# Moving the start addresses of TensorE's operands, and reading one weight with a step of two

## The chip, the core and the metric

The kernel runs on one core of one Trainium2 chip. The metric is the device time of one execution in microseconds; the figure for a kernel is the median of its runs. The kernel before takes 816.12 us (two runs, 815.71 and 816.52). The profiled execution shown here took 816.59 us.

## The reference

Three blocks in a row on 2304 tokens (batch 4 times 576) of width 512, all float32.

```python
# 1 attention with random features, 8 heads of 64, 128 features
h = omega @ (x * 64**-0.25) - |x|**2 / 2;  phi = exp(h - max(h)) / sqrt(128)      # for q and k
out = (phi_q @ (phi_k.T @ v)) / (phi_q @ sum(phi_k) + 1e-6)
# 2 feed-forward, 512 -> 2048 -> 512
x = softplus(x @ w_in) @ w_out
# 3 gated feed-forward, 512 -> 1024 -> 1024 -> 512
x = (((x @ w1) * (x @ w2)) @ w3) @ w_out2
```

## The kernel before

A float32 product is made of three products of `float32r` parts: an operand x is split into hi (x rounded by a copy to `float32r`) and lo (x minus hi), and `mm3` (L95 to L98) issues hi·hi, hi·lo and lo·hi into one accumulator. In each matmul one operand is the **stationary** one (128x128, loaded by a LDWEIGHTS that the trace shows under PEld), the other the **moving** one (256, 384 or 512 columns). In `mm3` the arguments `a` are the stationary parts and `b` the moving ones, so the three matmuls take stationary hi, hi, lo and moving hi, lo, hi.

The stages, in order of time:

- **Attention**: projections of k and q on omega (256 columns, stationary `kt` or `qt`, moving `om`), small float32 products, and transposes.
- **Up1** (class `Up1`, base `Quad`): x @ w_in in a scheme of seven products per 2x2 block. Stationary are the weight parts `hi`, `lo`, `thi`, `tlo` from pool `J_`; moving are token blocks of 384 columns from pools `X0` and `X1`. 1008 matmuls.
- **down** (function `down`): g @ w_out. Stationary is `w_out` in `X0`; moving are `dhi` and `dlo`, blocks of 512 columns (the last chunk 256) split from `dn` in pool `M_`. 768 matmuls of 512 columns and 192 of 256.
- **Up2**: as Up1, with the columns of w1 and w2. 1008 matmuls.
- **fold** (function `fold`, L878): w3 @ w_out2 is multiplied out first, as 8 row blocks. Stationary are w3's parts in `J_`, moving the 512 columns of w_out2 in `X1` (`spare` for the last of 8 blocks). 192 matmuls.
- **last** (function `narrow`): the gated product times the folded weight. Stationary and moving both lie in `X0` and `X1`. 504 matmuls of 384 columns.

SBUF is given out by pools, each a row of equal slots. The helper `mt` (L83) takes a slot of pool `M_` (14 slots of 2048 bytes in each partition), `jt` (L86) one of `J_` (8 slots of 4096 bytes). In the built program every operand of a `float32r` matmul, stationary or moving, starts at a multiple of 128 bytes. `lined` (L281) and the tile `edge` (L262) pad other tiles so that this holds.

The order of the instructions on each engine is set when the program is written (a list of small operations is pumped between matmuls at fixed rates, `step`); loads and stores go through SP's and ACT's DMA queues. The weights are laid out on the host (`_layout`); w3 arrives as rows of 1024 words, eight blocks of 128 one behind the other, and `fold` reads block i as `a:a + 128` with `a = 128 * i`.

Of the kernel before, what the change touches and what calls it, by code (L numbers as in the profile page):

```python
# [19 lines left out]
F32 = mybir.dt.float32  # L20
FR = mybir.dt.float32r
# [10 lines left out]
KD, NF, NJ = DM // 128, FF1 // 128, FF2 // 128  # L32
# [30 lines left out]
FILL = [18, 19, 20]  # L63
URGENT = 300
LINE = 32


@with_exitstack
def body(ctx: ExitStack, tc: tile.TileContext, q, k, k_rest, v, v_rest, om_t, w_in, w_out, w12, w3, wo, out):
    nc = tc.nc  # L70
    cp = ctx.enter_context(tc.tile_pool(name="cp", bufs=1))
    sm = ctx.enter_context(tc.tile_pool(name="sm", bufs=1))
    M_ = ctx.enter_context(tc.tile_pool(name="M_", bufs=14))
    L_ = ctx.enter_context(tc.tile_pool(name="L_", bufs=2))
    T_ = ctx.enter_context(tc.tile_pool(name="T_", bufs=4))
    J_ = ctx.enter_context(tc.tile_pool(name="J_", bufs=8))
# [3 lines left out]
    def ps():  # L80
        return ps_.tile([128, 512], F32, tag="ps", name="ps")

    def mt(n=512, dt=F32, name="m"):  # L83
        return M_.tile([128, n], dt, tag="m", name=name)

    def jt(name):  # L86
        return J_.tile([128, 1024], FR, tag="j", name=name)

    def tt(name):
        return T_.tile([128, 1024], F32, tag="t", name=name)  # L90
# [1 line left out]
    def matmul(o, a, b, start, stop, **kw):  # L92
        nc.tensor.matmul(out=o, lhsT=a, rhs=b, start=start, stop=stop, **kw)  # L93

    def mm3(o, ahi, alo, bhi, blo, first, last, **kw):  # L95
        matmul(o, ahi, bhi, first, False, **kw)
        matmul(o, ahi, blo, False, False, **kw)
        matmul(o, alo, bhi, False, last, **kw)  # L98
# [139 lines left out]
    def step(rate):  # L238
        due[0] += rate
        while due[0] > 0:  # L240
            if not pump_one():
                due[0] = min(due[0], 2.0)
                break
            due[0] -= 1

    def until(done):
        while not done():
            assert pump_one()
# [6 lines left out]
    for x in range(2):  # L255
        nc.vector.memset(bias[:, x:x + 1], BIAS * (2 * x - 1))
    win = [Job(w_in[i], 1024, jt, "J", True) for i in range(NF // 2)]
    w12_j = [Job(w12[i], 1024, jt, "J", True) for i in range(NJ)]


    edge = ctx.enter_context(tc.tile_pool(name="edge", bufs=1, side="right"))
    nc.gpsimd.memset(edge.tile([128, 24], F32, name="edge"), 0.0)  # L262
    qstack, kstack, x0stack = ExitStack(), ExitStack(), ExitStack()
    Q_ = qstack.enter_context(tc.tile_pool(name="Q_", bufs=1))
    K_ = kstack.enter_context(tc.tile_pool(name="K_", bufs=1, side="right"))
# [15 lines left out]
    def lined(pool, n, **kw):  # L281
        return pool.tile([128, -(-n // LINE) * LINE], F32, **kw)[:, :n]

# [68 lines left out]
    def k_feat_rest(r):  # L352
        kpr[r] = mt(name="kpr").rearrange("p (h m) -> p h m", h=4)
        p = project(lambda p: [krest[:, r, p, :]])
        waiting.append(lambda: features(*p, kpr[r]))
        flush(0)
# [118 lines left out]
    class Quad:  # L475
# [21 lines left out]
        def add(self, y, bank, name):  # L497
            z = mt(N, name=name)
            with tc.high_priority(URGENT):
                nc.vector.tensor_tensor(out=z, in0=bank, in1=y, op=ALU.add)  # L500
            return z

        def begin_parts(self):
            p6 = mt(N, name="p6")
            b1 = self.product("t2", "s2")
            with tc.high_priority(URGENT):
                nc.scalar.copy(out=p6, in_=b1)  # L507
            yield
            self.b2 = self.product("t3", "s3")
            yield  # L510
            self.b3 = self.product("t1", "s1")
            yield
            self.b0 = self.product("b11", "a11")
            self.u2 = self.add(p6, self.b0, "u2")
            u3 = self.add(self.u2, self.b2, "u3")
            self.c22 = self.add(u3, self.b3, "c22")
# [242 lines left out]
    for s in range(NW):  # L759
        n = min(WB, NF * 512 - WB * s)  # L760
# [63 lines left out]
    made, w34, xn = {}, {}, {}  # L824
# [41 lines left out]
    def w3_ops(j):  # L866
        return halves(w3f[j], 2, 2, "J", jt, ("w3", j))
# [10 lines left out]
    def fold(j):  # L878
        until(lambda: ("w3", j) in made)
        acc = ps()  # L880
        hi, lo = made["w3", j]
        for i in range(NJ):
            until(lambda: ("wo", i) in made)
            a = 128 * i
            mm3(acc, hi[:, a:a + 128], lo[:, a:a + 128], *made["wo", i], i == 0, i == NJ - 1)
            step(FOLD_RATE)
        o = mt(name="w34")
        with tc.high_priority(URGENT):
            nc.scalar.copy(out=o, in_=acc)
        free["J"] += 2  # L890
        return o
# [206 lines left out]
    for n, j in enumerate(order):  # L1098
        if 0 < n < NJ - 1:
            queue[:0] = w3_late.pop() + w3_next(n + 2)  # L1100
        rows[j] = fold(j)
        if n % 2:
            queue[:0] = w34_ops(n // 2, rows[order[n - 1]], rows[j])
# [8 lines left out]
def _layout(i):  # L1112
    import numpy as np

    def words(a):
        return np.ascontiguousarray(a).view(np.int64)

    q = i["q"].transpose(1, 3, 0, 2).reshape(4, 128, NT // 128, 128).transpose(2, 1, 0, 3)
    k = i["k"].transpose(0, 1, 3, 2).reshape(B, 2, 2, 128, S)
    k_main = k[..., :512].reshape(2 * B, 2, 128, 512).transpose(0, 2, 1, 3)  # L1120
    k_rest = k[..., 512:].reshape(B // 2, 2, 2, 2, 128, 64).transpose(4, 0, 2, 3, 1, 5).reshape(128, B, 2, 128)
    v = np.ones((B, 2, S, 4, D + 1), i["v"].dtype)
    v[..., :D] = i["v"].reshape(B, 2, 4, S, D).transpose(0, 1, 3, 2, 4)
    v_main = v[:, :, :512].reshape(2 * B, KT, 128, 4, D + 1).transpose(0, 2, 1, 3, 4)
    v_rest = v[:, :, 512:].reshape(B // 2, 2, 2, 64, 4, D + 1).transpose(1, 3, 0, 2, 4, 5).reshape(128, B, 4, D + 1)

    om = np.zeros((128, 2 * M), i["omega"].dtype)
    om[:D, :M] = om[D:, M:] = i["omega"].T

    def rows(w, n):  # L1130
        return w.reshape(-1, n, 128, w.shape[1]).transpose(0, 2, 1, 3).reshape(-1, 128, n * w.shape[1])

    def blocks(w, n):
        r, c = w.shape
        return w.reshape(r // 128, 128, c // 128 // n, n, 128).transpose(2, 1, 3, 0, 4).reshape(c // 128 // n, 128, -1)

    def quads(w):

        x = w.reshape(2, 2, 128, -1, 2, 128).transpose(3, 2, 0, 4, 1, 5)
        x = np.stack([x[:, :, 0, 0], x[:, :, 0, 1], x[:, :, 1, 1], x[:, :, 1, 0]], axis=2)  # L1140
        return x.reshape(x.shape[0], 128, 1024)

    w12 = np.stack([i["moe2_w1"].reshape(DM, NJ, 128), i["moe2_w2"].reshape(DM, NJ, 128)], axis=2).reshape(DM, -1)
    return {
        "q": np.ascontiguousarray(q),
        "k": np.ascontiguousarray(k_main),
        "k_rest": np.ascontiguousarray(k_rest),
        "v": np.ascontiguousarray(v_main),
        "v_rest": np.ascontiguousarray(v_rest),
        "om": om,  # L1150
        "w_in": words(quads(i["moe_w_in"])),
        "w_out": words(rows(i["moe_w_out"], NF)[0]),
        "w12": words(quads(w12)),
        "w3": words(blocks(np.ascontiguousarray(i["moe2_w3"].T), 1)),
        "wo": words(rows(i["moe2_w_out"], 1)),
    }

# [18 lines left out]
```

## Time and profile before

| | |
|---|---|
| time, median of 2 runs | 816.12 us (815.71 to 816.52) |
| profiled execution, its own time | 816.59 us |
| span in it, first to last instruction | 814.8 us |
| granted TensorE clock, mean | 0.999 |
| PE busy | 804.7 us, 99%, 5520 matmuls |
| PEld (weight loads) busy | 755.6 us, 93% |
| DVE busy | 594.1 us, 73% |
| ACT busy | 443.2 us, 54% |
| POOL busy | 43.7 us, 5% |

A matmul's duration in the trace runs from its start to its result, and matmuls overlap in it; a busy PE therefore says little on how fast it runs. What counts on a full PE is the **spacing**, the time from one matmul's start to the next one's: it is read from the first and the last start of a stretch and the number of matmuls between them.

### The profile page before, as it was taken

How to read it: one execution, taken by the hardware profiler on the slowest of the kernel's cores; microseconds unless marked ns; L12 is line 12 of the kernel's file. 1: busy time of each engine (PE TensorE's matmuls, PEld its weight loads, DVE VectorE, ACT ScalarE, POOL GpSimd, SP SyncE). 2: the span in 40 equal slices, each digit the busy share in tenths (PEclk: the TensorE clock that was granted, in tenths of full speed). 3: DMA queues.
4: the chain of work that ended last, by engine and by line, in shares of the span. 5: the costliest groups of instructions: out<-in, count | busy, mean ns of one | idle time of the engine just before them, and what ended most of it. 6: DMA issues, size and time to landing. Idle time of an engine off the chain costs nothing.

```text
span 814.8 us, 14545 instructions
## 1 busy us (share of the span) xinstructions
PE 804.7 (99%) x5520; PEld 755.6 (93%) x5520; DVE 594.1 (73%) x1005; ACT 443.2 (54%) x863; POOL 43.7 (5%) x38
## 2 busy tenths in 40 slices
PE   7999999999999999999999999999999999999998
PEld 6998989999999998888888889999999998889998
DVE  4888799878756666754569633898888866888861
ACT  6899998557545665755456422422334223674330
POOL 4623310000000000000000000000000000000000
PEclk9999999999999999999999999999999999999999
DMA  8733535756545457778984632455466556353212
GB/s 283 279 133 89 186 86 164 243 183 225 199 158 192 165 203 243 233 247 303 331 297 152 220 97 83 159 208 176 165 229 217 188 173 233 119 166 124 73 65 77
DMA packets 75717, 150.04 MB, mean 184 GB/s; under 512 B 7168, under 2 KB 44672, under 8 KB 75648
## 3 DMA queue, kind: packets, MB, share of 16 engines
q1 hardware_dynamic: 64560, 101.94, 37.6%
q10 hardware_dynamic: 11088, 47.18, 16.9%
q8 instruction: 43, 0.70, 0.4%
q14 instruction: 26, 0.21, 0.1%
HBM read 98.24 MB, written 50.86 MB: 183 GB/s over the span
## 4 chain that ended last, share of the span: by engine, by line
PE 85%; DVE 5%; ACT 4%; DMA 3%; issue 1%; SPq 0%; DVEq 0%; ACTq 0%
PE ps L93 84%; ACT kp L337 2%; DMA xq<-xd 1%; PE ps L390 1%; DVE s L445 1%; DMA raw<-in_w_in 1%; PE ps L420 1%; DVE nmax L332 1%; DVE xt L411 1%; ACT qp L337 1%; DVE qt L285 0%; DVE c L500 0%; DMA xd<-xs 0%; ACT f L135 0%; ACT raw L136 0%
## 5 line engine op out<-in xcount | busy, mean ns | idle before, releaser
L93 PE MATMUL ps<-dhi,lo 128*128 128x512 f32 (+1 forms) x320 | 117.7, 368 | 0.0
L93 PE MATMUL ps<-dlo,hi 128*128 128x512 f32 (+1 forms) x320 | 117.7, 368 | 0.0
L93 PE MATMUL ps<-dhi,hi 128*128 128x512 f32 (+1 forms) x320 | 117.5, 368 | 0.0
L621 DVE TENSOR_TENSOR dlo<-dn,dhi 128x512 fp32r<-128x512 f32 (+1 forms) x80 | 50.5, 635 | 48.4 <-ACT dhi L620 26.7
L620 ACT CAST dhi<-dn 128x512 fp32r<-128x512 f32 (+1 forms) x80 | 45.6, 576 | 56.9 <-DVE dlo L621 30.3
L500 DVE TENSOR_TENSOR c<-ps,u 128x384 f32<-128x384 f32 x144 | 71.4, 548 | 0.8
L93 PEld LDWEIGHTS ps<-dlo,hi 128*128 128x128 f32 x320 | 60.3, 189 | 10.1
L93 PEld LDWEIGHTS ps<-dhi,lo 128*128 128x128 f32 x320 | 60.3, 189 | 10.1
L93 PEld LDWEIGHTS ps<-dhi,hi 128*128 128x128 f32 x320 | 60.3, 189 | 9.8
L500 DVE TENSOR_TENSOR u<-ps,p 128x384 f32<-128x384 f32 x48 | 26.7, 555 | 58.0 <-PE ps L93 52.5
L135 ACT ACTIVATE f<-raw,bias 128x1024 f32<-128x1024 int16 (+2 forms) x43 | 46.6, 1090 | 33.5 <-DVE lo L176 8.5
L540 ACT ACTIVATE c<-c 128x384 f32<-128x384 f32 x72 | 35.0, 524 | 47.5 <-DVE c L500 47.5
L332 DVE TENSOR_REDUCE nmax<-ps 128x4 f32<-128x512 f32 x72 | 47.6, 680 | 17.8 <-PE ps L93 12.3
L139 DVE SCALAR_TENSOR_TENSOR f<-raw,f 128x1024 int32<-128x1024 f32 (+2 forms) x43 | 45.8, 1066 | 17.8 <-ACT raw L136 17.5
L507 ACT COPY p<-ps 128x384 f32<-128x384 f32 x48 | 22.9, 477 | 61.7 <-PE ps L93 52.6
L136 ACT ACTIVATE raw<-raw,bias 128x1024 f32<-128x1024 int16 (+2 forms) x43 | 46.3, 1082 | 0.4
L145 DVE SCALAR_TENSOR_TENSOR f<-raw,f 128x1024 int32<-128x1024 int32 (+2 forms) x43 | 45.0, 1046 | 0.6
L337 ACT ACTIVATE qp<-ps,nmax 128x128 f32<-128x128 f32 x144 | 42.8, 508 | 0.0
L337 ACT ACTIVATE kp<-ps,nmax 128x128 f32<-128x128 f32 x128 | 35.5, 489 | 8.2 <-DVE nmax L332 8.2
L93 PE MATMUL ps<-xs1h,thi 128*128 128x384 f32 x96 | 32.3, 336 | 0.3 <-DVE c L500 0.3
L93 PE MATMUL ps<-xs2h,thi 128*128 128x384 f32 x96 | 32.3, 336 | 0.0
L93 PE MATMUL ps<-xs2h,tlo 128*128 128x384 f32 x96 | 32.2, 335 | 0.0
(237 smaller groups left out, 2269.6 us busy)
## 6 DMA issues: line engine op xcount, KB each, us to landing
dn<-gd SPq DMA_DIRECT2D x64, 256.0 KB, 3.9
raw<-in_w ACTq DMA_DIRECT2D x16, 1023.8 KB, 5.2
gd<-c SPq DMA_DIRECT2D x80, 192.0 KB, 2.8
pd<-c SPq DMA_DIRECT2D x48, 192.0 KB, 2.5
raw<-in_w_out ACTq DMA_DIRECT2D x10, 767.8 KB, 4.6
raw<-in_w_in ACTq DMA_DIRECT2D x6, 1023.8 KB, 5.1
rawq<-in_q SPq DMA_DIRECT2D x18, 256.0 KB, 2.8
xd<-xs SPq DMA_DIRECT2D x18, 256.0 KB, 3.0
```

What stands on the lines that cost most here:

```text
L93: nc.tensor.matmul(out=o, lhsT=a, rhs=b, start=start, stop=stop, **kw)
L135: nc.scalar.activation(out=self.f, in_=top, func=AF.Relu, scale=TOP, bias=bias[:, 0:1])
L136: nc.scalar.activation(out=self.words(1, F32, 2), in_=top, func=AF.Identity, scale=TOP, bias=bias[:, 1:2])
L139: nc.vector.scalar_tensor_tensor(out=self.f.bitcast(I32), in0=self.words(1, F32, 2), scalar=-2.0 ** 31, in1=self.f, op0=ALU.max, op1=ALU.min)
L145: nc.vector.scalar_tensor_tensor(out=fi, in0=self.words(0, I32, 2), scalar=13, in1=fi, op0=ALU.logical_shift_right, op1=ALU.bitwise_or,)
L332: nc.vector.tensor_reduce(out=nmax, in_=pj, axis=AX.X, op=ALU.max, negate=True)
L337: nc.scalar.activation(out=dst[:, h, :], in_=pj[:, h, :], func=AF.Exp, bias=nmax[:, h:h + 1])
L500: nc.vector.tensor_tensor(out=z, in0=bank, in1=y, op=ALU.add)
L507: nc.scalar.copy(out=p6, in_=b1)
L540: nc.scalar.activation(out=dst, in_=src, func=AF.Softplus)
L620: nc.scalar.copy(out=hi, in_=got[m])
L621: nc.vector.tensor_tensor(out=lo, in0=got.pop(m), in1=hi.bitcast(F32), op=ALU.subtract)
```

## The change

Nothing is computed differently and no instruction is moved: on PE, DVE, ACT and SP the rows of the program and their waits are the same, in the same order. POOL has one more, a memset of a new tile `low` (128x8), which is never read. What changes is where tiles lie and how one weight is read:

- Slots of `M_` become 2080 bytes apart and those of `J_` 4128 (32 bytes more each). The 32 bytes of `low` and 768 bytes less of scratch for DMA move the starts of the pools behind them.
- w3's blocks are laid out in pairs, interleaved word by word, and `fold` reads a block of 128 words with a step of two words.

```diff
+OFF = 8
     def mt(n=512, dt=F32, name="m"):
-        return M_.tile([128, n], dt, tag="m", name=name)
+        return M_.tile([128, n + OFF * (n == 512)], dt, tag="m", name=name)[:, :n]
     def jt(name):
-        return J_.tile([128, 1024], FR, tag="j", name=name)
+        return J_.tile([128, 1024 + OFF], FR, tag="j", name=name)[:, :1024]
...
     nc.gpsimd.memset(edge.tile([128, 24], F32, name="edge"), 0.0)
+    low = cp.tile([128, 8], F32, name="low")
+    nc.gpsimd.memset(low, 0.0)
...
-            a = 128 * i
-            mm3(acc, hi[:, a:a + 128], lo[:, a:a + 128], *made["wo", i], i == 0, i == NJ - 1)
+            a = slice(256 * (i // 2) + i % 2, 256 * (i // 2 + 1), 2)
+            mm3(acc, hi[:, a], lo[:, a], *made["wo", i], i == 0, i == NJ - 1)
...
+    def pairs(w):
+        return w.reshape(NJ, 128, 4, 2, 128).transpose(0, 1, 2, 4, 3).reshape(NJ, 128, 1024)
...
-        "w3": words(blocks(np.ascontiguousarray(i["moe2_w3"].T), 1)),
+        "w3": words(pairs(blocks(np.ascontiguousarray(i["moe2_w3"].T), 1))),
...
-    nc = bacc.Bacc("TRN2", target_bir_lowering=False, num_devices=1, dynamic_dma_scratch_size=1024)
+    nc = bacc.Bacc("TRN2", target_bir_lowering=False, num_devices=1, dynamic_dma_scratch_size=256)
```

The starts in the built programs, in bytes past a multiple of 128 (all are 0 before):

| pool | now |
|---|---|
| `J_`, slots 0 to 7 | 96, 0, 32, 64, 96, 0, 32, 64; a weight of Up1 or Up2 takes four in a row: thi 96, tlo 0, hi 32, lo 64 |
| `M_`, slots 0 to 13 | 32, 64, 96, 0, 32, ...; dhi and dlo of one block lie in neighbouring slots |
| `Q_`, `L_`, `T_` | 96 |
| `X0`, `X1`, `K_`, `spare`, `ident` | 0, as before |

Taking 128 bytes as four quarters of 32, the `float32r` matmuls of the changed program stand so:

| stage | columns | stationary, moving | matmuls | both starts in the same quarter | in different ones |
|---|---|---|---|---|---|
| k projections | 256 | `K_`, `Q_` | 168 | 0 | 168 |
| q projections | 256 | `Q_`, `Q_` | 216 | 216 | 0 |
| Up1 and Up2 | 384 | `J_`, `X0` or `X1` | 2016 | 288 | 1728 |
| down | 512 | `X0`, `M_` | 768 | 164 | 604 |
| down, last chunk | 256 | `X0`, `M_` | 192 | 44 | 148 |
| fold (step of two) | 512 | `J_`, `X1` or `spare` | 192 | 32 | 160 |
| last | 384 | `X0` or `X1`, `spare` | 504 | 504 | 0 |
| sum | | | 4056 | 1248 | 2808 |

## Rows read from the trace of the kernel before

**Rows 1.** Page, part 1: busy us (share), instructions of each engine.
```profile
PE 804.7 (99%) x5520; PEld 755.6 (93%) x5520; DVE 594.1 (73%) x1005; ACT 443.2 (54%) x863; POOL 43.7 (5%) x38
```

**Rows 2.** Chain of waits in order of time: start us, us, what; its longest PE pieces.
```profile
153.64 565.96 PE ps L93 x3030
721.36 0.96 DVE s L981
726.26 85.24 PE ps L93 x490
```

**Rows 3.** Windows by stage: bounds, length, each engine's busy us (count), clock, DMA, GB/s.
```profile
155.00:308.00 153.00, 153.00 (x882) 152.49 (x881) 109.68 (x178) 91.83 (x153) 0.00 (x0) 1.00 0.57 196
309.00:482.00 173.00, 173.00 (x765) 143.24 (x764) 106.24 (x147) 92.12 (x133) 0.00 (x0) 1.00 0.71 236
506.00:679.00 173.00, 173.00 (x1000) 173.00 (x999) 141.98 (x244) 58.84 (x74) 0.00 (x0) 1.00 0.53 184
680.00:723.00 43.00, 43.00 (x191) 35.59 (x190) 31.30 (x56) 23.14 (x43) 0.00 (x0) 1.00 0.50 171
727.00:810.00 83.00, 83.00 (x481) 83.00 (x480) 59.05 (x82) 31.62 (x47) 0.00 (x0) 1.00 0.30 99
```

**Rows 4.** Timeline of PE, Up1, first and last of 31: start us, us, what.
```profile
259.70 0.33 PE L93 MATMUL ps<-xs4h,hi 128*128 128x384 f32 x1
259.88 0.33 PE L93 MATMUL ps<-xs4l,hi 128*128 128x384 f32 x1
...
264.90 0.33 PE L93 MATMUL ps<-xa11h,hi 128*128 128x384 f32 x1
```

**Rows 5.** Timeline of PE, down, first and last of 31.
```profile
315.13 0.39 PE L93 MATMUL ps<-dlo,hi 128*128 128x512 f32 x1
315.36 0.39 PE L93 MATMUL ps<-dhi,lo 128*128 128x512 f32 x1
...
321.93 0.39 PE L93 MATMUL ps<-dlo,hi 128*128 128x512 f32 x1
```

**Rows 6.** Timeline of PE, last chunk of down, first and last of 41.
```profile
486.02 0.28 PE L93 MATMUL ps<-dhi,lo 128*128 128x256 f32 x1
486.14 0.28 PE L93 MATMUL ps<-dhi,hi 128*128 128x256 f32 x1
...
490.82 0.28 PE L93 MATMUL ps<-dhi,hi 128*128 128x256 f32 x1
```

**Rows 7.** Timeline of PE, q projections, 23 matmuls from 53.78 to 56.40.
```profile
53.78 0.28 PE L93 MATMUL ps<-oml,qt 128*128 128x256 f32 x1
...
56.40 0.28 PE L93 MATMUL ps<-omh,qt 128*128 128x256 f32 x1
```

**Rows 8.** Timeline of PE, q projections of a later token block.
```profile
113.27 0.39 PE L93 MATMUL ps<-omh,qt 128*128 128x256 f32 x2
113.50 0.28 PE L93 MATMUL ps<-oml,qt 128*128 128x256 f32 x1
```

**Rows 9.** Timeline of PE, the first ten of down.
```profile
308.06 0.39 PE L93 MATMUL ps<-dhi,hi 128*128 128x512 f32 x1
308.29 0.40 PE L93 MATMUL ps<-dlo,hi 128*128 128x512 f32 x1
308.53 0.40 PE L93 MATMUL ps<-dhi,lo 128*128 128x512 f32 x1
...
310.15 0.39 PE L93 MATMUL ps<-dhi,hi 128*128 128x512 f32 x1
```

**Rows 10.** Timeline of PE, last stage after a wait, the second to the eighth.
```profile
726.54 0.33 PE L93 MATMUL ps<-xs2l,th 128*128 128x384 f32 x1
726.71 0.34 PE L93 MATMUL ps<-xs2h,tl 128*128 128x384 f32 x1
726.88 0.34 PE L93 MATMUL ps<-xs2h,th 128*128 128x384 f32 x1
...
727.60 0.33 PE L93 MATMUL ps<-xs2h,th 128*128 128x384 f32 x1
```

**Rows 11.** Groups of weight loads by form: count | busy us, mean ns | idle before.
```profile
L93 PEld LDWEIGHTS ps<-dhi,lo 128*128 128x128 f32 x320 | 60.3, 189 | 10.1
L93 PEld LDWEIGHTS ps<-xs2l,thi 128*128 128x128 f32 x96 | 18.0, 188 | 0.0
L93 PEld LDWEIGHTS ps<-hi,lo 128*128 128x128 f32 x56 | 10.5, 188 | 2.1
```

**Rows 12.** Page, part 6: a DMA's count, KB each, median us to landing.
```profile
dn<-gd SPq DMA_DIRECT2D x64, 256.0 KB, 3.9
```

## The prediction

> **What bounds the kernel now.** Part 1 of the page comes first: PE is busy 99% of the span, the next engine, DVE, 73% [rows 1]. That alone doesn't make PE the bound, since overlapping matmuls keep it "busy" at any speed. The chain of waits does: from 153.64 us it is PE for 565.96 us without a break, 3030 matmuls, and after a pause of a few us PE again for 85.24 us to the end [rows 2]. So from 154 us on nothing but the rate of matmuls sets the time. The windows show that the clock is no part of this: the granted clock is 1.00, the 2.4 GHz level, in every stage, and no other engine is full (DVE 109.68 of 153 us in Up1 and 141.98 of 173 us in Up2, the DMA engines 0.71 in down) [rows 3].
>
> The rate is read from starts. Up1: 30 steps of 384 columns in 5.20 us, 173.3 ns each [rows 4]. Down: 30 steps of 512 columns in 6.80 us, 226.7 ns [rows 5]. Its last chunk: 40 steps of 256 columns in 4.80 us, 120.0 ns [rows 6]. From 256 to 384 to 512 the spacing grows by 53.3 ns per 128 columns, one column per cycle at 2.4 GHz; taken back to no columns, **13.3 ns, 32 cycles, are left over in every matmul whatever its size**. Over the 4056 `float32r` matmuls that is 54 us. It is the only thing that this change can touch on PE, as the order of work and the waits stay the same.
>
> Is the 13.3 ns fixed? Not quite. The spacing of a stage that has just begun is another one: the first nine steps of down take 2.09 us, 232 ns each, before they fall into 226.7 [rows 9], and after a wait in the last stage six steps take 1.06 us, 176.7 ns [rows 10]. With 256 columns it goes the other way: 22 steps in the q projections take 2.62 us, 119.1 ns [rows 7], and two later ones 0.23 us, 115 ns each [rows 8]. In all of these the operands start at multiples of 128 bytes. So what a matmul loses depends on how the reads of its stream and of the next weights fall in time against each other, and the long stages have settled into a step in which that is the same each time. Addresses may act in the same way, but **no row of this trace has `float32r` operands at other starts**; their price has to be bounded.
>
> **The change, part by part.** The sum is made against the profiled execution's 816.6 us (span 814.8 us, 1.8 us around it), 0.5 us above the median of 816.12.
>
> *Stationary and moving starts in different quarters of 128 bytes*: 2808 matmuls, of them 1728 in Up1 and Up2, 604 + 148 in down, 160 in fold, 168 in the k projections. The price per matmul lies between two ends. Below: the whole left-over vanishes, -13.3 ns, 2808 x 13.3 = 37.3 us. Above: the settled step is lost, as in the rows after a stage's start, +5.3 ns at 512 columns and +3.4 ns at 384 [rows 4, 5, 9, 10]. Nearest to the new state, in which starts differ from one matmul to the next, are the rows out of step: those of 256 columns are 0.9 ns shorter on average and up to 5 ns [rows 7, 8], those of 384 and 512 longer. I take **-2 ns**, a choice between the -0.9 ns of the 256 columns and the middle of the two ends at 512, -4.0: 2808 x 2 = 5.6 us. As PE has no slack in these stages, all but the k projections' 0.3 us of it is on the path. The Trainium skill ("TensorE: Matmul & The Clock Gate", "Wait — 56ns, not 53.3ns?") gives warm matmuls in a row a left-over of about 2.5 ns; by it as the floor the term would be 2808 x 10.8 = 30.3 us and the time an estimate of 786 us, but no `float32r` row here comes near it.
>
> *The same quarter*: 1248 matmuls, the last stage's 504 and the q projections' 216 among them, cost what they did. Nothing.
>
> *w3 with a step of two*: 192 weight loads of 188 ns [rows 11] now span 1024 bytes of a partition in place of 512. They lie under matmuls spaced 226.7 ns, and a load starts with the matmul before it, so 39 ns more would still be hidden: nothing. The far end is a load that takes twice as long, 376 ns: then it sets the spacing, 149 ns more, 192 x 149 = 28.7 us. I take nothing, since the count of words read is the same and the nearest rows, all unstepped, are 188 or 189 ns at any place.
>
> *Transfers, DVE and ACT at the new starts*: `dn` lands 3.9 us after its issue [rows 12] and is asked for four blocks ahead, 4 x 12 x 226.7 ns = 10.9 us; doubled it would still be early. DVE and ACT in down are busy 106 and 92 of 173 us [rows 3]; 10% more on either stays under PE. Both nothing; without that cover the next late thing would be `dlo` in down.
>
> *`low` and its memset*: one on POOL, at the start, 5% busy [rows 1]. Nothing.
>
> Sum: 816.6 - 5.6 = **811 us**.
>
> If PE runs faster, what is late next? Down would have to lose 67 us before DVE's 106 us bounded it, Up2 31 us before DVE's 142 us. No case below takes that much.
>
> **The rivals.**
>
> *Nothing happens* (the 13.3 ns belong to the matmul and not to addresses). For it: three sizes have exactly the same left-over. Against it: rows 7 to 10 show other spacings with the same operands' starts. Time 816.6 us. The Trainium skill ("TensorE: Matmul & The Clock Gate", "Step-by-step: what each phase is for") says that stream and weights are read through two independent ports and that loading weights takes no bandwidth from the running matmul; by it starts can't matter and this case holds. The spacings out of step speak against so plain a reading.
>
> *A clear gain*: the reads no longer meet in most of the 2808. From the shortest spacing that I see, -5 ns [rows 8], 2808 x 5.0 = 14.0 us, to the whole left-over, 37.3 us: 803 down to 779, middle 791 us. For it: 32 cycles in each matmul is what one lost cycle per 16 bytes of a 512-byte weight would give, and different quarters are kept in 21 of 25 matmuls of Up1 and Up2 (1728 of 2016). Against it: no matmul of the trace has less than half of it.
>
> *The step is lost* (slower). All long stages run settled; a matmul that follows at a changed start may never settle. In down the moving start changes with every matmul, in Up1 and Up2 the stationary one with every product. Price: Up1 and Up2 2016 x 3.4 = 6.9 us, down and fold 960 x 5.3 = 5.1 us, together 12.0 us: 829 us. It decides as soon as fewer than about half of the matmuls settle at the old spacing or below. For it: ten matmuls pass before down settles [rows 9], and a product of Up1 is only six long. Against it: in Up1 each product brings another moving tile without any trace of it [rows 4], though at equal starts.
>
> *The stepped load becomes the bound* of fold: 28.7 us, 845 us. Against it speaks the count of words, which is the same.
>
> **How the numbers follow.** Chances: small gain (811 us) 0.30; clear gain 0.23; nothing 0.20; step lost 0.22; stepped load 0.05. The predicted time is the likeliest case's, 811 us. Its own range is 805 to 815 us. The two signs hold nearly as much each, so the range for 8 in 10 spans cases: it reaches up to the lost step at its full price, 829 us, which leaves out the stepped load and a little more, 0.07; and down to 793 us, past the shallower half of the clear gain, which leaves out 0.12. This kernel's runs agree far better than 2%, but 2% is the bound for the three chances: below 800 us, within, above 832 us. Faster takes three quarters of the clear gain, whose shallow end I hold for the likelier, 0.17. Slower takes the stepped load and the tail of the lost step, 0.07. The rest, 0.76, is within 2%.
>
> **What would show it.** In the changed kernel's timeline, read start to start: Up1 near 171 ns on average in place of 173.3, and uneven inside a triple, since stationary hi, hi, lo lie in two quarters; products of thi/tlo (96 and 0) unlike those of hi/lo (32 and 64). Down near 225 ns, uneven by d and block. Last stage at 173.3, q projections as before. Fold's PEld near 188 ns; if it shows over 227, the stepped load bounds. If down shows 230 ns or more, the step is lost. All spacings equal to today's to the tenth: nothing happens. I would be wrong in kind if the starts acted on the moving stream alone (Up1 and Up2 unchanged, only down moved), or if a wait of PE on DVE or a DMA appeared in 155 to 720 us, where there is none now.

## The result and the profile after

The changed kernel takes **825.81 us** (median of 2 runs, 825.59 to 826.03) against 816.12 us: slower by a ratio of 1.0119, interval 1.0075 to 1.0162. The forecast was 811 us, on the other side; its range, 793 to 829, holds the time. The span grew from 814.8 to 824.2 us.

Part 1 of the page (busy us, share, instructions) looks as it did, which answers [rows 1]:

```profile
PE 814.3 (99%) x5520; PEld 760.9 (92%) x5520; DVE 594.4 (72%) x1005; ACT 443.4 (54%) x863; POOL 43.7 (5%) x39
```

The longest piece of the chain of waits (start us, us, what), against [rows 2], is still matmuls without a break. It now runs through to PE's last matmul:

```profile
154.78 666.16 PE ps L94 x3552
```

The pause in [rows 2] was one of the chain and not of PE: fold's and the last stage's matmuls went on through it, and the longest step from one start to the next there was 0.48 us (0.33 us now).

The windows by stage (columns as in [rows 3]) show the clock at its upper level, 2.4 GHz, and every other engine no busier than it was:

```profile
155.00:308.00 153.00, 153.00 (x872) 152.60 (x872) 108.17 (x176) 91.29 (x154) 0.00 (x0) 1.00 0.55 193
312.00:486.00 174.00, 174.00 (x752) 140.95 (x751) 105.36 (x144) 91.64 (x132) 0.00 (x0) 1.00 0.71 234
511.00:686.00 175.00, 175.00 (x1003) 175.00 (x1002) 141.92 (x243) 59.58 (x76) 0.00 (x0) 1.00 0.52 182
738.00:820.00 82.00, 82.00 (x475) 82.00 (x474) 57.79 (x80) 30.27 (x44) 0.00 (x0) 1.00 0.28 94
```

In Up1's window PE has 872 matmuls in 153 us where there were 882: the rate fell, not the occupation. The rate itself is read from starts again. Timeline of PE in Up1, the first and the last of 31 matmuls, and in the same way down, which answer to [rows 4, 5]:

```profile
261.88 0.34 PE L94 MATMUL ps<-xs4h,hi 128*128 128x384 f32 x1
...
267.14 0.34 PE L94 MATMUL ps<-xa11h,hi 128*128 128x384 f32 x1
...
325.01 0.40 PE L94 MATMUL ps<-dlo,hi 128*128 128x512 f32 x1
325.24 0.40 PE L94 MATMUL ps<-dhi,lo 128*128 128x512 f32 x1
...
331.98 0.39 PE L94 MATMUL ps<-dlo,hi 128*128 128x512 f32 x1
```

30 steps of 384 columns take 5.26 us, 175.3 ns each (173.3 before); 30 steps of 512 take 6.97 us, 232.3 ns (226.7 before). The last chunk of down, 40 steps, answers to [rows 6], and 18 steps of the last stage stand below it:

```profile
493.86 0.28 PE L94 MATMUL ps<-dhi,hi 128*128 128x256 f32 x1
...
498.61 0.28 PE L94 MATMUL ps<-dlo,hi 128*128 128x256 f32 x1
...
737.56 0.33 PE L94 MATMUL ps<-xa11h,bh 128*128 128x384 f32 x1
...
740.68 0.33 PE L94 MATMUL ps<-xa11h,bh 128*128 128x384 f32 x1
```

256 columns became shorter, 4.75 us over 40 or 118.8 ns against 120.0. The last stage, whose operands did not move, has 3.12 us over 18, 173.3 ns. In fold, 30 steps take 7.02 us, 234.0 ns:

```profile
690.11 0.40 PE L94 MATMUL ps<-hi,lo 128*128 128x512 f32 x1
...
693.15 0.64 PE L94 MATMUL ps<-spare,hi 128*128 128x512 f32 x2
...
697.13 0.39 PE L94 MATMUL ps<-hi,lo 128*128 128x512 f32 x1
```

Weight loads by form (count, busy us and mean ns, idle before), against [rows 11]: down, Up, and fold with its step of two.

```profile
L94 PEld LDWEIGHTS ps<-dhi,lo 128*128 128x128 f32 x320 | 60.1, 188 | 11.3
L94 PEld LDWEIGHTS ps<-xs2l,thi 128*128 128x128 f32 x96 | 18.0, 188 | 0.0
L94 PEld LDWEIGHTS ps<-hi,lo 128*128 128x128 f32 x56 | 10.9, 195 | 2.2
```

The stepped load takes 195 ns, under a spacing of 234: it does not bound.

Where the time went, by the first matmul of each stage in both traces:

| stage | before, us | after, us | difference | matmuls | per matmul |
|---|---|---|---|---|---|
| all ahead of Up1 | 122.99 | 124.21 | +1.22 | | |
| Up1 | 181.06 | 182.70 | +1.64 | 1008 of 384 | +1.6 ns |
| down | 174.12 | 178.03 | +3.91 | 768 of 512 | +5.1 ns |
| last chunk | 23.03 | 22.74 | -0.29 | 192 of 256 | -1.5 ns |
| Up2 | 174.73 | 176.64 | +1.91 | 1008 of 384 | +1.9 ns |
| fold | 43.56 | 44.86 | +1.30 | 192 of 512 | +6.8 ns |
| last | 87.64 | 87.48 | -0.16 | 504 of 384 | |

The sum is 9.5 us, from the first matmul to the last. The 1.22 us ahead of Up1 are no part of the effect that I can show: that stretch took 122.72 and 123.98 us in two of the kernels below in which its operands' starts do not differ from one another. The remaining 8.3 us are nearly all matmul spacing. A little of it is not: Up1's single wait near 154 us is a step of 0.63 us before and of 0.45 us after, so Up1's +1.64 us is a little less than its spacings lost, and the last stage's -0.16 us is the shorter step named above.

### The profile page after: what moved, and what is told of

The parts are those of the page before. It is cut to its first block, busy times and chain, and to the rows that moved or that the text cites. A ratio compares the mean times of both kernels' runs of the same rounds, so it can differ in the third digit from the quotient of the medians.

```text
span 824.2 us, 14546 instructions
## 1 busy us (share of the span) xinstructions
PE 814.3 (99%) x5520; PEld 760.9 (92%) x5520; DVE 594.4 (72%) x1005; ACT 443.4 (54%) x863; POOL 43.7 (5%) x39
## 4 chain that ended last, share of the span: by engine, by line
PE 86%; DVE 5%; ACT 3%; DMA 3%; issue 0%; SPq 0%
PE ps L94 84%; ACT kp L340 2%; DMA xq<-xd 1%; PE ps L393 1%; DVE s L448 1%; DMA raw<-in_w_in 1%; DVE nmax L335 1%; DVE xt L414 1%; PE ps L423 1%; ACT qp L340 1%; DVE c L503 0%; DMA xd<-xs 0%; DVE qt L288 0%; ACT f L136 0%; ACT raw L137 0%; DVE u L503 0%
## 5 line engine op out<-in xcount | busy, mean ns | idle before, releaser
L94 PE MATMUL ps<-dhi,lo 128*128 128x512 f32 (+1 forms) x320 | 118.8, 371 | 0.0
L94 PE MATMUL ps<-xs4h,lo 128*128 128x384 f32 x96 | 32.6, 340 | 0.0
L94 PE MATMUL ps<-xa11h,lo 128*128 128x384 f32 x96 | 32.5, 339 | 0.0
```

## The experiments

**The theory** after the result: a matmul whose weights and stream start at different places within 128 bytes does not settle into the step of the long stages, and then its spacing is that of [rows 9, 10]. Settled means: at the spacing that matmuls of that width hold in the kernel before. **Rivals**: the place itself matters (an operand that is not at a multiple of 128 is read slower); only the moving stream matters; the step of two costs fold its time; what matters is that starts change from one matmul to the next.

### The moving slots alone

```diff
-        return M_.tile([128, n], dt, tag="m", name=name)
+        return M_.tile([128, n + OFF * (n == 512)], dt, tag="m", name=name)[:, :n]
```

with two small tiles, one behind `M_`, that keep the other pools at multiples of 128.

> Only the slots of M_ turn through the four quarters (2080 bytes apart); J_, L_, T_, Q_ start at multiples of 128 and w3 is read without a step. Theory A (a settled step needs every matmul's operands to start at the same place as the last one's; otherwise a matmul pays the spacing out of step): down at about 231.8 ns instead of 226.7, its last chunk near 118.5 instead of 120.0, Up1 and Up2 at 173.3, fold at 226.7; +3.9 - 0.3 = about 819.7 us. Theory B (a start in another quarter than the other operand's costs by itself): the same for down, 604 of 768 differ, but the 164 in the same quarter should stay at 226.7, so about 230.7 on average and 819 us. If Up1 or fold move as well, neither holds.

Measured: 821.3 us (820.43 to 821.73, 4 runs), ratio 1.0047, interval 1.0029 to 1.0066. Timeline of PE in down, the first and last of 31:

```profile
329.85 0.39 PE L95 MATMUL ps<-dlo,hi 128*128 128x512 f32 x1
...
336.78 0.39 PE L95 MATMUL ps<-dlo,hi 128*128 128x512 f32 x1
```

6.93 us over 30 steps, 231.0 ns. The whole of down takes 178.02 us, as in the full change (178.03), and the last chunk 22.75. Up is at 173.4 ns. The trace also has one wait of PE on DVE in Up2, a gap of 0.83 us between two starts at one place, which the full change does not have.

### The weight slots alone

```diff
-        return J_.tile([128, 1024], FR, tag="j", name=name)
+        return J_.tile([128, 1024 + OFF], FR, tag="j", name=name)[:, :1024]
```

again with small tiles that keep the other pools at multiples of 128.

> Only the slots of J_ turn (96, 0, 32, 64); M_ and Q_ start at multiples of 128, w3 is read without a step. Theories A and B: Up1 and Up2 near 176 ns (+3.5 us), fold between 231 and 234 ns (+1 us), down at 226.7: about 821 us. A says further that matmuls whose two starts share a quarter are as slow as the others; B that they keep 173.3. If down moves, neither holds. If the stationary operand's start did not matter, Up would be at 173.3 and the time 816 us.

Measured: 821.0 us (820.58 to 822.16, 4 runs), ratio 1.0049, interval 1.0033 to 1.0066. Timeline of PE in Up1, the first and last of 31:

```profile
259.90 0.34 PE L96 MATMUL ps<-xs4h,hi 128*128 128x384 f32 x1
...
265.15 0.33 PE L96 MATMUL ps<-xa11h,hi 128*128 128x384 f32 x1
```

175.0 ns in place of 173.3. Up1 and Up2 together are 3.1 us longer and fold 0.9 us, while down has its 174.1 us of before. So a moved stationary start acts as a moved moving one does: "only the moving stream matters" falls. The two parts' 4.4 us (against the 816.95 us of before on the same chip) and 4.0 us add up to most of the whole.

### The step of two alone

```diff
-            a = 128 * i
-            mm3(acc, hi[:, a:a + 128], lo[:, a:a + 128], *made["wo", i], i == 0, i == NJ - 1)
+            a = slice(256 * (i // 2) + i % 2, 256 * (i // 2 + 1), 2)
+            mm3(acc, hi[:, a], lo[:, a], *made["wo", i], i == 0, i == NJ - 1)
```

> Only w3's blocks are interleaved and read with a step of two words; all slots as in the kernel before, so that a block starts 0 or 4 bytes past a multiple of 128. If only the starts count (A and B alike): fold near 226.7 ns, 816 us. If the step itself disturbs the settled pattern: fold at 232 to 234 ns, +1.2 us, 817.3 us. If the stepped load took twice as long: fold at 376 ns, 845 us; the changed kernel's fold at 233.7 ns speaks against that already.

Measured: 817.55 us (817.03 to 819.69, 10 runs), ratio 1.0008, interval 0.9997 to 1.0019: not told apart from before by its time. The trace tells more. Fold, 31 steps (one row in between holds two):

```profile
690.28 0.39 PE L93 MATMUL ps<-spare,lo 128*128 128x512 f32 x1
...
697.52 0.39 PE L93 MATMUL ps<-hi 128*128 128x512 f32 x1
```

7.24 us, 233.5 ns each, and the stage takes 44.79 us, 1.23 more than before. The weight tiles lie at multiples of 128 bytes here, so fold leaves its settled spacing without any moved slot. But every second block of w3 now starts one word, 4 bytes, further, and the two blocks alternate every three matmuls: whether the step or these 4 bytes do it, this kernel does not separate. Fold's 44.86 us in the full change is nearly reached already, and the moved weight slots add next to nothing to it, though alone they cost 0.9 us: the two costs do not add up. The weight loads take 193 ns.

### One constant difference of 32 bytes

No slot grows; one tile of 32 bytes is put in front, so that all left pools (`J_`, `M_` and others) lie 32 past a multiple of 128 and `X0` and `X1` stay. Every matmul of Up, down and fold then has its two starts 32 apart, always the same way.

```diff
+OFF = 8
+    low = cp.tile([128, OFF], F32, name="low")
+    nc.gpsimd.memset(low, 0.0)
```

> No slot gets longer; M_, L_, T_, J_ and Q_ all start 32 bytes past a multiple of 128, in every slot alike, while X0, X1 and K_ stay at 0. So in Up1, Up2, down and fold every matmul has its two operands in different quarters, but always in the same two. Theory A: the step settles as before, Up 173.3, down 226.7, fold 226.7 ns, 816 us. Theory B: all 2016 + 960 matmuls differ, more than in the changed kernel, so Up 176 or more, down 232, fold 233 ns, 826 us or more. If a constant difference lets the reads pass each other better, the settled spacing is below 173.3 and the time below 816 us.

Measured: 824.08 us (822.34 to 824.66, 4 runs), ratio 1.0081, interval 1.0063 to 1.0100. Timeline of PE: 30 steps each of Up1, of down and of the last chunk.

```profile
259.98 0.34 PE L94 MATMUL ps<-xa22h,tlo 128*128 128x384 f32 x1
...
265.18 0.34 PE L94 MATMUL ps<-xs1h,tlo 128*128 128x384 f32 x1
...
329.84 0.40 PE L94 MATMUL ps<-dhi,hi 128*128 128x512 f32 x1
...
336.84 0.40 PE L94 MATMUL ps<-dhi,hi 128*128 128x512 f32 x1
...
491.89 0.28 PE L94 MATMUL ps<-dhi,hi 128*128 128x256 f32 x1
...
495.40 0.28 PE L94 MATMUL ps<-dhi,hi 128*128 128x256 f32 x1
```

173.3, 233.3 and 117.0 ns. For 512 columns a constant difference costs more than the changing one (down 179.19 us against 178.03): the rival that changing starts are what hurts falls for them. For 384 columns it stands: at a constant 32 they settle, and fall back to 173.3 ns after each of this trace's waits in Up.

### Everything 32 bytes off, with no difference

```diff
+    low = cp.tile([128, OFF], F32, name="low")     # ahead of all pools on the left
+    nc.gpsimd.memset(low, 0.0)
-    nc.gpsimd.memset(edge.tile([128, 24], F32, name="edge"), 0.0)
+    nc.gpsimd.memset(edge.tile([128, 16], F32, name="edge"), 0.0)
```

> Every pool, on both sides of SBUF, starts 32 bytes past a multiple of 128, so that stationary and moving operand are again in the same quarter everywhere, but no operand starts at a multiple of 128. Theory D (what counts is the difference of the two starts): as the kernel before, Up 173.3, down 226.7, its last chunk 120.0, fold 226.7 ns, 816.5 us. Theory P (what counts is the place itself, multiples of 128 being good for 512 columns): down and fold near 233.3 ns as with the constant 32 bytes on one side, +5.1 + 1.3 us, 823 us.

Measured: 816.95 us (816.28 to 820.28, 10 runs), ratio 1.0008, interval 0.9997 to 1.0019. Timeline of down, 30 steps in 6.80 us, 226.7 ns:

```profile
319.96 0.39 PE L94 MATMUL ps<-dhi,hi 128*128 128x512 f32 x1
...
326.76 0.39 PE L94 MATMUL ps<-dhi,hi 128*128 128x512 f32 x1
```

Down, last chunk, Up2 and fold take 174.12, 23.03, 174.73 and 43.56 us, the figures of before to the last digit. This decides against the place itself: a start 32 bytes past the multiple of 128 is as good as one at it, and what costs in down and fold is **the difference of the two starts**. No cost on DVE, ACT or the DMAs, whose tiles moved with the rest, shows in these stages either.

### A constant difference of 64 bytes

As the constant 32, with `OFF = 16`.

> As the kernel with a constant 32 bytes, with 64: M_, L_, T_, J_, Q_ start 64 bytes past a multiple of 128 in every slot, X0, X1 and K_ at 0. If 384 columns settle at any constant difference: Up 173.3 ns; if the difference matters there too: near 175.0 ns, +3.4 us. If 512 columns settle only at no difference: down and fold near 233.3 ns and the time near 823 us; if half of 128 bytes serves as well as none (the settled starts in the trace of before fall at two points of time, half a period apart): 226.7 ns and 816.5 us.

Measured: 822.43 us (821.05 to 823.01, 4 runs), ratio 1.0063, interval 1.0046 to 1.0080. Down, 30 steps:

```profile
330.01 0.39 PE L94 MATMUL ps<-dhi,hi 128*128 128x512 f32 x1
...
336.87 0.39 PE L94 MATMUL ps<-dhi,hi 128*128 128x512 f32 x1
```

228.7 ns here, between the settled 226.7 and the 233.3 of a constant 32, while fold in the same run is at 233.3 (44.80 us). In down the moving operand lies at 64 and the weights at 0; in fold it is the other way round.

Up has no single spacing in this trace. Up1 runs at 173.3 ns from 141 to 153 us, at 174.7 behind a step there that is 27 ns longer, and at 176.7 behind three longer steps at 176 to 178 us up to its end at 310 us. Timeline of PE in Up1, 30 steps in 5.30 us:

```profile
259.91 0.34 PE L94 MATMUL ps<-xa22l,thi 128*128 128x384 f32 x1
...
265.21 0.34 PE L94 MATMUL ps<-xs1l,thi 128*128 128x384 f32 x1
```

Up2 runs at 174.7 ns up to a wait of PE on DVE at 632.84 us, and at 173.3 from there on. The starts are the same all the time; the spacing changes where the matmuls go on after a wait or a delay. The next but one kernel shows it again. The 175.2 ns in the table below is a mean over these steps.

### Two starts for the weights, 32 and 96

```diff
+        a = OFF * name.endswith("hi")
-        return J_.tile([128, 1024], FR, tag="j", name=name)
+        return J_.tile([128, 1024 + OFF], FR, tag="j", name=name)[:, a:a + 1024]
```

This was meant to give the two weights of one product (`thi` with `tlo`, `hi` with `lo`) one start, so that it changes between products and not inside a triple. As built it does not. The pool gives out its eight slots in falling order: a weight of Up takes the slots 0, 7, 6, 5 or 4, 3, 2, 1 for `thi`, `tlo`, `hi`, `lo`. So they start at 32, 96, 96, 32 here, and every triple still changes its start. For the same reason the starts in the changed kernel are `thi` 96, `tlo` 64, `hi` 32, `lo` 0, and not `tlo` 0 and `lo` 64, as was said ahead of the prediction and in it; the table's 288 matmuls of Up with both starts in one quarter are those with `lo` (`tlo` has 384).

> J_'s slots lie 4128 bytes apart, but hi and thi use the last 4096 of theirs and lo and tlo the first, so that the two stationary parts of one product start alike: thi and tlo at 32, hi and lo at 96. The start changes only from one kind of product to another, every 6 or 12 matmuls, no longer within a triple; M_ stays at multiples of 128, w3 without a step. If it is the change from matmul to matmul that keeps Up from settling: Up at 173.3 to 174 ns, at most +1 us for it; fold, whose starts are constant over a block of 24 matmuls, at 233 ns (+1.2 us) if 512 columns settle only without a difference; together about 818 us. If 384 columns do not settle at 96 bytes of difference, or each change of product costs a new settling: Up near 175 ns or more, +3 us, 821 us.

Measured: 821.2 us (820.32 to 822.24, 4 runs), ratio 1.0053, interval 1.0038 to 1.0068. Up2, 30 steps in 5.25 us, 175.0 ns:

```profile
559.98 0.34 PE L95 MATMUL ps<-xa11l,hi 128*128 128x384 f32 x1
...
565.23 0.34 PE L95 MATMUL ps<-xs3l,thi 128*128 128x384 f32 x1
```

Up is as slow as in the full change, 175.2 ns over both stages, with two starts in place of four. That agrees with the case that a start which changes inside the triple keeps Up from settling, but does not test it: no kernel here changes its start between products alone.

### A constant 96 bytes with the step of two

As the constant 32 with `OFF = 24`, and w3 in pairs with the step of two.

> As the kernel with a constant 32 bytes, with 96, and w3 read with a step of two words as in the changed kernel. Up 173.3 ns if 384 columns settle at any constant difference, else near 175.0. Down near 233.3 ns if 512 columns settle only without a difference. Fold with step and difference: 233 ns, since neither alone leaves it settled; if the pair were what lets weights and stream pass each other, it would be below 226.7. Time 822 to 824 us.

Measured: 823.33 us (821.68 to 824.97, 2 runs), ratio 1.0078, interval 1.0050 to 1.0106. Down and fold are at 233.3, and the 256 columns of the last chunk are back at a mean of 120.0, in steps that alternate between 116 and 125. Up1 is settled at 173.3 ns, and so is Up2 up to a wait of PE on DVE, a step of 1.13 us. Timeline of PE in Up2: 30 steps before that wait, the matmul behind it, and 30 steps after.

```profile
559.96 0.34 PE L94 MATMUL ps<-xs1h,thi 128*128 128x384 f32 x1
...
565.16 0.34 PE L94 MATMUL ps<-xs2h,thi 128*128 128x384 f32 x1
...
611.88 0.45 PE L94 MATMUL ps<-xs1h,thi 128*128 128x384 f32 x1 [0.79 <-DVE c L503]
...
639.90 0.34 PE L94 MATMUL ps<-xs2h,tlo 128*128 128x384 f32 x1
...
645.20 0.34 PE L94 MATMUL ps<-xs4h,lo 128*128 128x384 f32 x1
```

5.20 us ahead of it, 173.3 ns each, and 5.30 us after it, 176.7 ns each, up to the end of Up2. So with its starts 64 or 96 apart a stream of 384 columns holds one of several steps, and a wait can move it to another. With equal starts, or 32 apart, Up came back to 173.3 ns after every wait of the traces here.

### Only what gains: 32 bytes between the operands of 256 columns

```diff
+        a = OFF * (n == 256 and dt == FR)
-        return M_.tile([128, n], dt, tag="m", name=name)
+        return M_.tile([128, n + a], dt, tag="m", name=name)[:, a:]
-    om_s = [Q_.tile([128, 2 * M], FR, name=f"om{x}") for x in "hl"]
+    om_s = [Q_.tile([128, 2 * M + LINE], FR, name=f"om{x}")[:, OFF:OFF + 2 * M] for x in "hl"]
```

> From what the runs so far show: equal starts are best where 384 and 512 columns run, a constant difference of 32 bytes where 256 do (116.7 ns instead of 120.0 in the last chunk of down with the constant 32 bytes). Here only the moving operands of 256 columns, dhi and dlo of the last chunk and om's two parts, start 32 bytes past a multiple of 128; all else is as in the kernel before. Last chunk at 116.7 ns, -0.63 us; k and q projections near 117 ns, of which part lies under waits for ACT and DVE, -0.3 to -0.8 us; Up 173.3, down 226.7, fold 226.7 as before. Together -0.9 to -1.4 us, 0.1 to 0.2%, about 815.4 us beside 816.6: at the edge of what five rounds tell. If the whole effect depends on what ran before, 120 ns and no change.

Measured: 815.74 us (814.78 to 817.8, 11 runs) against 816.59 (15 runs), ratio 0.9992, interval 0.9983 to 1.0001. The last chunk, 30 steps in 3.50 us:

```profile
484.94 0.28 PE L95 MATMUL ps<-dhi,hi 128*128 128x256 f32 x1
...
488.44 0.28 PE L95 MATMUL ps<-dhi,hi 128*128 128x256 f32 x1
```

116.7 ns; the chunk takes 22.40 us, 0.63 less. That gain is plain in the trace, but the whole kernel's is not clear of the runs' scatter. Its median is the lowest of all versions.

### Fold alone, moving operand 16 and 64 bytes off

```diff
-        parts_ = [halves(wof[i], 1, 2, "X1", lambda name: xslot("X1", 512, FR, name), ("wo", i)) for i in range(NJ - 1)]
+        parts_ = [halves(wof[i], 1, 2, "X1", lambda name: xslot("X1", 512 + OFF, FR, name)[:, OFF:], ("wo", i)) for i in range(NJ - 1)]
```

and the `spare` tiles likewise, with `OFF` 4 and 16. Weights stay at 0. One run each.

> Only the moving operands of fold (wo's parts) start 16 bytes past a multiple of 128, stationary at 0, no step. If the difference of starts counts in finer parts than 32 bytes: fold near 233.3 ns, +1.2 us. If only the quarter of 128 bytes counts: settled at 226.7 ns. A spacing below 226.7 would be a better step than any so far.

> Only the moving operands of fold start 64 bytes past a multiple of 128, stationary at 0. In the kernel with a constant 64 bytes down (moving 64, stationary 0) ran at 228.9 ns and fold (moving 0, stationary 64) at 233.3. If it is which operand is ahead that makes them differ: fold now near 228.9 ns. If it is the place of the tiles or the stage: 233.3 ns.

Measured: 819.06 us with 16 bytes, 817.25 us with 64, one run each. Fold, 31 steps with 16 bytes, then 31 with 64:

```profile
692.86 0.39 PE L94 MATMUL ps<-lo,hi 128*128 128x512 f32 x1
...
700.04 0.40 PE L94 MATMUL ps<-hi,lo 128*128 128x512 f32 x1
```

```profile
692.87 0.39 PE L94 MATMUL ps<-hi,lo 128*128 128x512 f32 x1
...
699.98 0.39 PE L94 MATMUL ps<-hi 128*128 128x512 f32 x1
```

7.18 us or 231.6 ns, and 7.11 us or 229.4 ns. 16 bytes apart are already enough to unsettle fold. And with the *moving* operand ahead by 64, fold is near down's 228.7 of the constant 64, not at its own 233.3 with the weights ahead: at 64 bytes it matters which of the two operands leads. Each of these figures is one stage in one trace; that the step was set by the way the stage began, as in Up, is not ruled out.

### All spacings together

Mean ns from start to start over the whole stage, waits left out. For 384 columns the last two rows are means over different steps: Up1 and Up2 have 176.1 and 174.3 at the constant 64, 173.4 and 174.8 at the constant 96.

| kernel | Up, 384 | down, 512 | last chunk, 256 | fold, 512 |
|---|---|---|---|---|
| before; everything 32 off | 173.4 | 226.7 | 120.0 | 226.9 |
| after | 175.3 | 231.8 | 118.5 | 233.7 |
| moving slots alone | 173.4 | 231.8 | 118.5 | 227.0 |
| weight slots alone | 175.2 | 226.7 | 120.0 | 231.7 |
| step of two alone | 173.4 | 226.7 | 120.0 | 233.3 |
| constant 32 | 173.4 | 233.3 | 116.7 | 233.5 |
| constant 64 | 175.2 | 228.9 | 117.8 | 233.3 |
| constant 96, step of two | 174.1 | 233.3 | 120.0 | 233.3 |

## Why the prediction was wrong

**What bounds** was right: PE's rate of matmuls sets the time from 154 us on, before and after, at the same clock and with no new wait. So was that PE has no slack in these stages: what the spacings lost is the time lost.

**The step that failed** is the price of different quarters, "-2 ns" on 2808 matmuls, -5.6 us. Measured on the stages: +5.1 ns in down, +6.8 in fold, +1.8 on average in Up1 and Up2, and -1.5 only in the last chunk. Two readings led there. First, the 13.3 ns left over was taken for a loss that new starts would rather reduce: the lower end of -13.3 ns, which no row came near, drew the middle to -4.0. Settled, the left-over is 13.3 ns at every width (120.0, 173.3, 226.7 ns). Out of step it grows with the width: the 256 columns stand at 116.7 ns and the 512 at 233.3 with a constant 32, 10.0 and 20.0 ns over their columns at 2.4 GHz, and the 384 at 175.3 in the changed kernel, 15.3 over. So being out of step gains below some width and costs above it. Those are not the only steps (174.7 and 176.7 ns for 384 columns and 228.9 for 512 stand for whole stretches of a stage), but none found for 384 or 512 columns is below the settled one.

Second, the signs of all three widths stood in the trace of before: 115 and 119.1 for 256 [rows 7, 8], 176.7 for 384 [rows 10], 232 for 512 [rows 9]. The prediction mixed them: it leaned on the 256 columns, which are 316 of its 2808 matmuls, and put their sign on 1728 of 384 and 764 of 512. Each term should have been priced from the row of its own width. That gives the rival that had only 0.22.

**The rival "the step is lost"** is what happened; the sign named for it, down at 230 ns or more, came with 232.3. Its 12.0 us were too large where they counted Up at the full price of [rows 10]: 6.9 us forecast, 3.55 measured. A step of 3.4 ns more does exist for 384 columns, 176.7 ns over a stretch of Up at a constant 64 and at a constant 96, but the changed kernel's starts, which differ from one matmul to the next, came to less than 2. Down and fold were 5.1 us forecast and 5.21 measured, which is partly luck: down was forecast at 4.1 and took 3.91, fold at 1.0 and took 1.30. The upper end of the range, which is this rival's full price, is all that lets it hold the 825.81 us; the term that was forecast has no part in it. The objection to it, that Up1 gets another moving tile with each product and stays settled [rows 4], was beside the point: those starts are all equal in their difference.

**"The same quarter: nothing"** held for the last stage (173.3 ns), where all matmuls are so. In down and fold it failed: the matmuls of those stages whose weights to come start in the same quarter as their stream have 231.05 ns in the changed kernel, little less than the 232.0 of the other matmuls of down and far from 226.7. What a matmul takes follows from the run of matmuls, not from its own two starts alone.

**The step of two** was costed at nothing on the ground that the count of words is the same. The load itself nearly held: 193 ns with the step alone and 195 in the full change against 188, hidden as said. But fold went from 226.9 to 233.3 ns with the step alone (and the 4 bytes that come with it), 1.2 us, through the spacing of the matmuls. The "stepped load bounds" case did not occur.

**"Nothing happens"** fell. That two kernels with the same instructions, one with every operand 32 bytes off and one with half of them, stand at ratios of 1.0008 and 1.0081 speaks against streams and weights that have nothing to do with each other. The Trainium skill ("TensorE: Matmul & The Clock Gate", "Step-by-step: what each phase is for") gives TensorE two independent read ports, one for the stream and one for the weights; the traces here do not agree with what I drew from it, that starts can't matter, and the measurement decides. What the two reads do to each other no run shows. The case "clear gain" fell with the sign; its shallow end of -5 ns was two steps read to 0.01 us, and the shortest spacing that holds over a stage is 116.7 ns, -3.3. The idea of one lost cycle per 16 bytes of a weight fits the settled 32 cycles, but no run tests it or shows a way to less than 10 ns.

**The covers**: DVE, ACT, the DMAs and the memset at nothing were right, by the kernel with everything 32 off, whose time is that of before to 0.1%.

## What to carry to other kernels

In a stream of `float32r` matmuls of 384 columns or more, give stationary and moving operands the same start within 128 bytes (0 and 32 were alike) and read weights without a step; with 256 columns a constant difference of 32 bytes is a little better (116.7 ns against 120.0). Where the starts differ, do not take a spacing from one stretch for the stage's: the same operands ran at 173.3 ns ahead of a wait and at 176.7 behind it. Price a change of such a stream from rows of the same width, each with its own sign: the few matmuls after a stage's start or after a wait show what the stream costs when it is not settled. And where all of an engine's time is one repeated instruction, a nanosecond of its spacing, read from first to last start, is worth more than any share of busy time.

## What the runs showed of the hardware

- Spacing of `float32r` matmuls at 2.4 GHz depends on the difference of the two operands' starts: 226.7 ns at 0, 231.4 at 16 bytes (fold), 233.3 at 32 and 96, 228.9 at 64 with the moving operand ahead and 233.3 with the weights ahead, all for 512 columns, one or two stages each.
- The widths do not agree on which differences settle: at a constant 32, 384 columns settle (173.4) and 512 do not (233.3).
- At one constant difference of 64 or 96 bytes, 384 columns hold steps of 173.3, 174.7 or 176.7 ns over stretches of 12 to 130 us, and change from one to another behind waits or single longer steps, the smallest 27 ns; with equal starts or 32 bytes apart they came back to 173.3 after every wait.
- Weights read with a step of two words, every second block 4 bytes further: 193 ns a load in place of 188, and 6.4 ns more of matmul spacing at 512 columns.
- Left open: what the two reads collide on, if they do, why the order of the operands matters at 64 bytes, how a wait picks the step, and whether Up's 1.8 ns comes from changes inside a triple or between products. The start of Up1 scatters by up to 2.9 us between all these kernels (122.14 to 125.07 us after the first matmul), and Up2 has one wait on DVE, a step of 0.7 to 1.1 us, in five of them (moving slots alone, constant 32, constant 64, constant 96, fold with 16 bytes); where these come from was not followed.
